# Top-k attention with a feed-forward block on one core: a first batch in single tiles, a regular conversion of the weights, and small operations put elsewhere

## The chip, the core and the metric

The kernel runs on one core of a Trainium2 chip. A core has five engines with a queue of instructions each, worked off in order: TensorE (PE in the profile; its weight loads are PEld), VectorE (DVE), ScalarE (ACT), GpSimd (POOL) and SyncE (SP), which here only issues DMAs. The metric is the time of one execution on the device, in microseconds (us). TensorE accumulates into PSUM; ScalarE copies from there to SBUF.

## The reference

There are 8 batches, 8 heads, 576 rows and 64 columns per head. Attention keeps, in every row of scores, those that are not below the 32nd largest. The result passes through a feed-forward block with a residual.

```python
scores = scale * np.matmul(q, k.transpose(0, 1, 3, 2))
kth = np.partition(scores, -top_k, axis=-1)[..., -top_k:-top_k + 1]
scores = np.where(scores >= kth, scores, -1000000000.0)
attn = np.exp(scores - np.max(scores, axis=-1, keepdims=True))
attn = attn / (np.sum(attn, axis=-1, keepdims=True) + 1e-09)
x = np.matmul(attn, v)            # then (B, H, S, D) -> (B, S, 512)
xn = (x - mu) / np.sqrt(var + 1e-06) * g_ln
out = x + np.maximum(xn @ w_ch1, 0.0) @ w_ch2     # 512 -> 2048 -> 512
```

The two weight matrices arrive as 64-bit floats, and the kernel converts them itself.

## The kernel before

**Units.** Two heads (a head pair `hp`, four of them) are worked on together. The 576 rows of queries are four tiles of 128 (`qt` 0 to 3) and a rest of 64 (`qt` = `J` = 4). A *unit* is one such tile of one head pair: two score tiles of 128 x 576, one per head; for the rest, one tile that holds both heads. A *job* is a batch, a head pair and a list of tiles. In batch 0 the lists are [0, 1] and [2, 3, J], from batch 1 on [0, 1, J] and [2, 3]; a list is done for all four head pairs before the next list. So there are 160 units in a fixed order.

**Steps.** The program is written as a loop over steps `n` (line numbers in the listing below), and there is no scheduler: each engine gets its instructions in the order in which the loop writes them. In step n, unit n is selected on VectorE, while its neighbours are at other stages:

- `scores` makes the scores of unit n+1 on TensorE (L362); ScalarE copies them from PSUM (L345).
- `select` finds the 32 largest of unit n in four rounds of MAX8 and MATCH_REPLACE8 (L379, L384). `select(u, 0)` to `select(u, 3)` stand at four places in the step; between them stands the other work.
- `prepare` and `mask` work on unit n-1: GpSimd adds a large negative number where a score is below the threshold (L409 compares, L412 adds). While weights are being converted, units are `shared`: for one of their two tiles ScalarE does the comparison (L399, L400), and GpSimd only subtracts (L407).
- `weigh` is the exponential of unit n-2 on ScalarE (L419), with the row sum into `den`; `turn` transposes it (L434, L463 on TensorE, copies L446 and L464).
- `values` multiplies the whole list by v when the list's last unit is n-3 (L487, L494; `oT`, L499), and `place` transposes back (`xo`, L526) and divides by `den` (`put`, L503, on ScalarE). The reciprocal of `den` is VectorE's (L782); an epsilon is added first, on GpSimd (L823).
- after the last head pair, `stats` takes mean and variance of the finished rows (L551, L552, VectorE), `std` the root (ScalarE), `inverse` the reciprocal (L561).

**Blocks.** Two finished row tiles are a block. `give` puts its matmuls into the list `todo`: `turn_x` (transposes, copied as `xT`, L576 and L581), 64 `hidden` (L589) and 32 `project` (L606), and each of the eight `fill` calls of a step pops as many as the plan's share allows, by estimated costs. The plan spreads a block over the steps up to the next block: windows of 12 and of 8 steps in turn. What is left then is popped at once. Behind the first list of batches 3 and 7 a second block comes on top, made of the rests of four batches.

**Weights.** Each of 32 *pieces* is fetched on SP, split by ScalarE into size, low part and sign (L168 to L172) and clamped on GpSimd (L173), shifted on VectorE (L176), and joined by two operations of GpSimd (L182, L183). Four pieces come before the loop, two in each of steps 0 to 9, and one a step until step 17. After four pieces of the first matrix `mean_of` forms a mean on TensorE and `centre` corrects the weights on VectorE (L223).

**Buffers** that matter: five PSUM banks `ps` for scores, transposes, `av` and `xo`; three `mm` for `hidden` and `project`; single input buffers `kin`, `qin`.

Of the kernel before, what the change touches and what calls it, by code (L numbers as in the profile page):

```python
# [20 lines left out]
J = 4  # L21
# [7 lines left out]
def kernel(  # L29
# [51 lines left out]
    NV = 3  # L81
# [19 lines left out]
    hpool = pool("h", NF - 1)  # L101
# [30 lines left out]
    class Piece:  # L132
# [26 lines left out]
        def split(self):  # L159
# [6 lines left out]
            self.sign = tmp("sign", FP32)  # L166
# [13 lines left out]
        def join(self):  # L180
            size = self.size[:]
            nc.gpsimd.tensor_tensor(size, size, self.low[:].bitcast(U32), ALU.add)  # L182
            nc.gpsimd.tensor_tensor(  # L183
                self.dst, size.bitcast(FP32), self.sign[:], ALU.mult
            )
            ready[self.i] = True

    ready = [False] * (2 * NF)
    centred = [False] * (DFF // DM)
# [3 lines left out]

    def load_gain():
        grow = const([NC, P], "grow")
        nc.scalar.dma_start(grow[:], g_ln.rearrange("(c p) -> c p", p=P))
# [23 lines left out]
    def centre(nb):  # L220
# [6 lines left out]
        centred[nb] = True  # L227
# [4 lines left out]
    for n in range(-1, 2 * NF):  # L232
        size = 4 if n < 0 else 2 if n < 10 else 1
        batches[n], queue = queue[:size], queue[size:]

    def weights(n, phase):

        now, before = batches.get(n, []), batches.get(n - 1, [])
        done = [x.i // NC for x in before if x.i < NF and x.c == NC - 1]
        if phase == 0:  # L240
            for x in batches.get(n + 1, []):
                x.fetch()
            for x in now[0::2]:
                x.split()
        elif phase == 1:
            for x in before:
                x.shift()
            for x in before[0::2]:
                x.join()
        elif phase == 2:  # L250
            for x in now[1::2]:
                x.split()
            for x in before[1::2]:
                x.join()
            for nb in means:
                if not centred[nb]:
                    centre(nb)
        elif phase == 3:
            for nb in done:
                mean_of(nb)  # L260
# [6 lines left out]

    def pop():
        cost, run, may = todo.pop(0)
# [4 lines left out]
    def fill():  # L274
        owed[0] = min(owed[0] + share[0], 6.0)
        while todo and owed[0] >= todo[0][0] / 2 and (not todo[0][2] or todo[0][2]()):
# [11 lines left out]
    def load(job, other):  # L288

        job.ins = {}  # L290
        for name, src, queue in (("k", k, nc.sync), ("q", q, other)):
# [47 lines left out]
    def scores(u):  # L339
# [3 lines left out]
        for s, pss in enumerate(made):  # L343
            for t, ps in enumerate(pss):
                nc.scalar.copy(u.sc[:, t, s * HALF : (s + 1) * HALF], ps[:, 0:HALF])  # L345
# [192 lines left out]
    class Block:  # L538
# [25 lines left out]
        def items(self):  # L564
# [38 lines left out]
            def project(i, f):  # L603
# [9 lines left out]
                if f == NF - 1:  # L613
# [7 lines left out]
            out = [(0.66, lambda i=i: turn_x(i), None) for i in range(n)]  # L621
            out += [
                (
                    max(per_row * N, 0.31),
                    lambda f=f, c=c: hidden(f, c),
                    lambda f=f: centred[f * P // DM],
                )
                for f in range(NF)
                for c in range(NC)
            ]  # L630
            out += [
                (
                    per_row * DM,
                    lambda i=i, f=f: project(i, f),
                    lambda f=f: ready[NF + f] and (f < NF - 1 or self.ready),
                )
                for i in range(n)
                for f in range(NF)
            ]
            return out  # L640

# [6 lines left out]
    for b in range(B):  # L648
        lo, hi = list(range(J // 2)), list(range(J // 2, J))
        (lo if b else hi).append(J)  # L650
        for qts in (lo, hi):
# [32 lines left out]
    for j in jobs:  # L684
        if j.hp == NHP - 1:
# [4 lines left out]
            add_block(step, tiles, [[(out[b, t[1] * P : (t[1] + 1) * P, :], full)] for t in tiles])  # L690
# [19 lines left out]
    turns = {}  # L710
    for j in fresh[1:]:
        before = jobs[jobs.index(j) - 1]
        turns[before.first] = j
# [21 lines left out]
    def give(n):  # L735
        while todo:
            pop()
        owed[0] = 0.0
        for blk in gives[n]:
            todo.extend(blk.items())  # L740
        after = [m for m in gives if m > n]
        steps = range(n, min(after) if after else END)
        need = sum(t[0] for t in todo)
# [7 lines left out]
    load(fresh[0], nc.scalar)  # L751
    weights(-2, 0)
    turn_heads(fresh[0])
    load(fresh[1], nc.sync)
    scores(units[0])
    load_gain()
    load_values(jobs[0])
    weights(-1, 0)
# [123 lines left out]
```

## Time and profile before

| | |
|---|---|
| median of three runs | 1772.06 us (1770.77 to 1772.45) |
| the profiled execution | 1770.78 us, span 1768.3 us |
| TensorE busy (PE) | 1635.9 us, 93% of the span |
| VectorE busy (DVE) | 1521.8 us, 86% |
| GpSimd busy (POOL) | 1208.3 us, 68% |
| ScalarE busy (ACT) | 969.3 us, 55% |
| a MAX8, a MATCH_REPLACE8 over 576 columns | 746 ns, 742 ns |
| the mask's comparison, its addition (GpSimd) | 2215 ns, 1409 ns |

The share of the span is a mean over stages with different limits, so the profile is read by stretches. A row of the windows view gives a stretch's start, end and length, and for each engine the busy time and the number of instructions, then the granted TensorE clock, the DMA share and GB/s. A line of a timeline gives start, duration, engine, line, operation, what is written and read, and in brackets the idle time before it and who ended it. In a waits line stand the total, the number of waits and the longest one.

### The profile page before, as it was taken

To read this page: it belongs to the slowest core of one execution; us is meant where nothing else is said; L and a number is where in the kernel's file an instruction comes from. 1 tells how busy PE (TensorE), PEld (TensorE's weight loads), DVE (VectorE), ACT (ScalarE), POOL (GpSimd) and SP (SyncE) were. 2 spreads that over 40 slices of the span, in tenths; PEclk is the share of its full clock that TensorE was granted. 3 is DMA by queue.
4 is the path that set the end of the run, shared out by engine and by line. 5 is a ranking of instruction groups with operands and counts; after the bars stand their busy time and mean duration, and the time that the engine had idled before them with its cause. 6 is when DMAs were issued, how large, how long until landed. Compare 5 with 4: busy or idle time off the path is not lost.

```text
span 1768.3 us, 23805 instructions
## 1 busy us (share of the span) xinstructions
PE 1635.9 (93%) x7617; PEld 1034.6 (59%) x7617; DVE 1521.8 (86%) x3162; ACT 969.3 (55%) x2563; POOL 1208.3 (68%) x959
## 2 busy tenths in 40 slices
PE   3555999999999999999999999999999999999998
PEld 1223746657574757575756575647575756566765
DVE  7888999999999999996569999999999999996000
ACT  4658876556564646553356565656565646544411
POOL 4869787787777777873467877777778776883300
PEclk9677999999999999999999999999999999999999
DMA  7423112101210012001021012101120021000000
GB/s 173 103 69 97 54 31 51 28 26 28 46 28 20 24 37 54 20 14 38 15 39 28 26 28 53 21 20 27 34 53 21 20 40 34 14 26 14 6 13 12
DMA packets 244485, 65.53 MB, mean 37 GB/s; under 512 B 235653, under 2 KB 235657, under 8 KB 244361
## 3 DMA queue, kind: packets, MB, share of 16 engines
q1 hardware_dynamic: 241984, 63.73, 16.2%
q8 instruction: 60, 0.98, 0.2%
q10 hardware_dynamic: 2376, 0.30, 0.1%
q14 instruction: 65, 0.52, 0.1%
HBM read 54.53 MB, written 9.44 MB: 36 GB/s over the span
## 4 chain that ended last, share of the span: by engine, by line
DVE 41%; PE 35%; POOL 9%; issue 9%; ACT 5%; DMA 1%; POOLq 0%; SPq 0%; DVEq 0%; ACTq 0%
DVE m L379 21%; DVE wk L384 18%; PE hps L589 13%; PE ops L606 11%; PE scps L362 4%; PE av L487 3%; PE tp L434 3%; POOL e L409 2%; POOL w L183 2%; POOL size L182 2%; POOL e L412 2%; ACT sc L345 1%; POOL e L407 1%; PE av L494 1%; POOL size L173 1%
## 5 line engine op out<-in xcount | busy, mean ns | idle before, releaser
L409 POOL TENSOR_SCALAR e<-sc,m 128x576 f32<-128x576 f32 x270 | 598.2, 2215 | 239.4 <-DVE m L379 170.9
L379 DVE MAX8 m<-wk 128x8 f32<-128x576 f32 x864 | 612.6, 746 | 2.1
L589 PE MATMUL hps<-xT,w 128*128 128x256 f32 x2304 | 556.9, 385 | 27.5 <-ACT xT L581 27.5
L606 PE MATMUL ops<-w,h 128*128 128x512 f32 x1152 | 544.0, 596 | 0.0
L589 PEld LDWEIGHTS hps<-xT,w 128*128 128x128 f32 x2304 | 419.5, 192 | 93.8 <-ACT xT L581 31.8
L384 DVE MATCH_REPLACE8 wk<-m,wk 128x576 f32<-128x576 f32 x576 | 423.7, 742 | 0.0
L412 POOL TENSOR_TENSOR e<-e,sc 128x576 f32<-128x576 f32 x270 | 380.3, 1409 | 22.6
L606 PEld LDWEIGHTS ops<-w,h 128*128 128x128 f32 x1152 | 199.3, 191 | 162.5 <-issue 157.4
L419 ACT ACTIVATE e<-e,bias 128x576 f32<-128x576 f32 x288 | 225.3, 782 | 57.5 <-POOL e L412 55.4
L345 ACT COPY sc<-scps 128x288 f32<-128x288 f32 x576 | 191.8, 415 | 97.9 <-PE scps L362 94.7
L379 DVE MAX8 m<-sc 128x8 f32<-128x576 f32 x288 | 203.1, 742 | 40.1 <-ACT sc L345 40.0
L362 PE MATMUL scps<-kT,qT 64*128 64x288 f32 (+3 forms) x1344 | 223.1, 435 | 9.3 <-DVE qT L321 8.1
L446 ACT COPY pt<-tp 128x512 f32<-128x512 f32 x256 | 150.3, 588 | 138.3 <-PE tp L434 136.8
L434 PE MATMUL tp<-ident,e 128*128 128x128 f32 x1152 | 178.0, 278 | 49.8 <-ACT e L419 49.8
L434 PEld LDWEIGHTS tp<-ident,e 128*128 128x128 f32 x1152 | 143.7, 143 | 126.7 <-ACT e L419 62.4
L384 DVE MATCH_REPLACE8 wk<-m,sc 128x576 f32<-128x576 f32 x288 | 211.9, 742 | 0.0
L362 PEld LDWEIGHTS scps<-kT,qT 64*128 64x128 f32 (+1 forms) x1344 | 126.5, 182 | 131.0 <-issue 59.7
L601 ACT ACTIVATE h<-hps 128x256 f32<-128x256 f32 x288 | 110.4, 384 | 159.5 <-PE hps L589 158.6
L487 PE MATMUL av<-pt,vb 128*64 128x256 f32 (+1 forms) x1024 | 141.2, 419 | 0.3
L616 POOL TENSOR_TENSOR o<-o,x 128x512 f32<-128x512 f32 x32 | 40.7, 1273 | 126.0 <-ACT o L615 125.7
L487 PEld LDWEIGHTS av<-pt,vb 128*64 128x64 f32 x1024 | 69.2, 139 | 66.5 <-issue 19.7
L503 ACT ACTIVATE x<-xo,den 128x64 f32<-128x64 f32 x256 | 59.3, 316 | 72.4 <-DVE den L782 39.2
(71 smaller groups left out, 1020.9 us busy)
## 6 DMA issues: line engine op xcount, KB each, us to landing
raw<-in_moe_w_ch_dram SPq DMA_DIRECT2D x32, 512.0 KB, 3.9
vb<-in_v_dram SPq DMA_DIRECT2D x128, 128.0 KB, 2.4
kin<-in_k_dram SPq DMA_DIRECT2D x128, 72.0 KB, 2.4
qin<-in_q_dram SPq DMA_DIRECT2D x124, 72.0 KB, 2.4
out_dram<-o SPq DMA_DIRECT2D x32, 256.0 KB, 2.1
ends<-in_v_dram SPq DMA_DIRECT2D x128, 16.0 KB, 2.1
dr<-den SPq DMA_DIRECT2D x64, 0.2 KB, 1.8
out_dram<-o SPq DMA_DIRECT2D x8, 128.0 KB, 2.4
```

What stands on the lines that cost most here:

```text
L345: nc.scalar.copy(u.sc[:, t, s * HALF : (s + 1) * HALF], ps[:, 0:HALF])
L362: nc.tensor.matmul(ps[i * R : i * R + ql, o : o + width], qT[r, q0 : q0 + ql], kT[r, k0 : k0 + width], start=True, stop=True,)
L379: nc.vector.max(m[:, t, :], u.cur[t])
L384: nc.vector.match_replace(u.wk[t][:], m[:, t, :], u.cur[t], LOWEST)
L409: nc.gpsimd.tensor_scalar(e, sc, u.thr[:, t, 7:8], MASKED, ALU.is_lt, ALU.mult)
L412: nc.gpsimd.tensor_tensor(e, e, sc, ALU.add)
L419: nc.scalar.activation(u.e[:, t], u.e[:, t], AF.Exp, bias=u.bias[:, t : t + 1], scale=scale, accum_out=g.den[:, col : col + 1],)
L434: nc.tensor.transpose(ps[:, c * P : (c + 1) * P], u.e[:, t, c * P + t * R : (c + 1) * P + t * R], ident[:],)
L446: nc.scalar.copy(g.pt[:, t * J : (t + 1) * J, q0 : q0 + P], ps[:].rearrange("p (c n) -> p c n", n=P),)
L487: nc.tensor.matmul(av[h * D : (h + 1) * D, 0 : g.nq], vb[:, h * J + c, :], g.pt[:, h * J + c, 0 : g.nq], start=(c == 0), stop=False,)
L589: nc.tensor.matmul(ps["h"][:, 0:N], w1[:, c, f * P : (f + 1) * P], xT[0][:, c, 0:N], start=(c == 0), stop=(c == NC - 1),)
L606: nc.tensor.matmul(ps["o"][:], hT[f][:, i * P : (i + 1) * P], w2[:, f, :], start=(f == 0), stop=(f == NF - 1),)
```

## The change

- **Order of batch 0.** The lists are [0], [1], [2, 3] and [J]; batch 1 has [0, 1] and [2, 3, J]; the later batches are as before. Batch 0 so has blocks of one tile (given in steps 7 and 11) and of two (step 19); the next come in steps 31 and 43, where before they came in 11, 23, 35 and 43.
- **Conversion.** None before the loop, then two pieces in every step 0 to 15; the shift moves behind the next step's `select(u, 0)`, the joins to phase 1, `mean_of` a step later. Units 0 to 15 are `shared`. A piece's sign lies in the `o` and `r` pools.
- **A readiness rule.** A block's matmul may be popped only in a step after the one in which its weights were made. While weights are missing, `give` doesn't empty `todo`, and puts new rows and `hidden` before the projections; later it may leave up to eight projections.
- **ScalarE and GpSimd.** Both exponentials of unit n-2 and `prepare` stand before `scores`; the copies go tile by tile; `mask` does both tiles at once, tile 1 first.
- **Small operations.** The epsilon is added on VectorE, and add and reciprocal stand behind `select(u, 1)` and the transposes of heads instead of behind `select(u, 0)`. `inverse` comes a step later.
- **Loads.** The first two jobs' heads are transposed before the loop, the others two steps ahead of their job; values are loaded near the end of a step, into two buffers instead of three.

```diff
-    NV = 3
+    NV = 2
-    hpool = pool("h", NF - 1)
+    hpool = pool("h", NF)
@@ weights
-        size = 4 if n < 0 else 2 if n < 10 else 1
+        size = 0 if n < 0 else 2
...
         if phase == 0:
             for x in batches.get(n + 1, []):
                 x.fetch()
+            for x in before:
+                x.shift()
             for x in now[0::2]:
                 x.split()
         elif phase == 1:
             for x in before:
-                x.shift()
-            for x in before[0::2]:
                 x.join()
-        elif phase == 2:
             for x in now[1::2]:
                 x.split()
-            for x in before[1::2]:
-                x.join()
+            for x in batches.get(n - 2, []):
+                if x.i < NF and x.c == NC - 1:
+                    mean_of(x.i // NC)
+        elif phase == 2:
...
+    def done(step):
+        return step is not None and step < now[0]
@@ jobs
-        lo, hi = list(range(J // 2)), list(range(J // 2, J))
-        (lo if b else hi).append(J)
-        for qts in (lo, hi):
+        parts = [[0], [1], [2, 3], [J]]
+        if b:
+            parts = [[0, 1], [2, 3]]
+            parts[b < 2].append(J)
+        for qts in parts:
@@ turns
-    turns = {}
-    for j in fresh[1:]:
-        before = jobs[jobs.index(j) - 1]
-        turns[before.first] = j
+    turns = {j.first - 2: j for j in fresh[2:]}
@@ give
-        while todo:
+        early = not all(map(done, ready))
+        while todo and not early and (len(todo) > 8 or todo[0][0] != "project"):
             pop()
...
+            kept = [i for i in todo if i[0] != "project"]
+            last = [i for i in todo if i[0] == "project"]
+            if early:
+                todo[:] = kept + rows + hidden + last + project
+            else:
+                todo[:] = kept + rows + last + hidden + project
...
+        if early:
+            plan.update({m: 1.2 for m in steps})
+            return
@@ the loop over steps
-        if u and n == u.job.first and n > 0:
-            load_values(u.job)
         if ex:
-            weigh(ex, 0)
+            for t in range(len(ex.tiles)):
+                weigh(ex, t)
+        if mk:
+            prepare(mk)
         if nxt:
             scores(nxt)
+        if n == 0:
+            load_gain()
         if g:
             values(g)
         if u:
             select(u, 0)
-        for den in recips.pop(n, []):
-            nc.vector.reciprocal(den, den)
         if mk:
-            prepare(mk)
-            mask(mk, 0)
+            for t in reversed(range(len(mk.tiles))):
+                mask(mk, t)
         weights(n, 0)
         fill()
-        if ex and len(ex.tiles) > 1:
-            weigh(ex, 1)
...
             turn_heads(turns[n])
...
+        for den in recips.pop(n, []):
+            nc.vector.tensor_scalar_add(den, den, DEN_EPS)
+            nc.vector.reciprocal(den, den)
         for blk in gives.get(n - 1, []):
             blk.std()
-        if mk and len(mk.tiles) > 1:
-            mask(mk, 1)
         weights(n, 1)
...
-        for blk in gives.get(n - 1, []):
+        for blk in gives.get(n - 2, []):
             blk.inverse()
...
-            nc.gpsimd.tensor_scalar_add(den, den, DEN_EPS)
...
+        if mk and mk.job.last == n - 1:
+            load_values(mk.job)
```

## The prediction

> **What bounds the kernel now.** I read the 40 slices first, then who waited for whom, then single steps. I call *step n* the stretch that begins with VectorE's first MAX8 on unit n (the row `m<-sc`). Steps 0, 20, 43, 54, 63 and 83 begin at 10.9, 257.7, 473.4, 570.0, 660.9 and 902.5 us.
>
> ```profile
> span 1768.3 us, 23805 instructions
> ...
> PE   3555999999999999999999999999999999999998
> ...
> DVE  7888999999999999996569999999999999996000
> ```
>
> TensorE starves for about 180 us. Then TensorE and VectorE are both full, except in two stretches where TensorE alone is (near 800 us and from 1575 us on). The same by steps (us, then PE, PEld, DVE, ACT, POOL busy, clock, DMA):
>
> ```profile
> 10.90:257.70 246.80, 159.28 (x662) 92.15 (x662) 220.62 (x429) 169.11 (x418) 188.73 (x160) 0.82 0.32 82
> 257.70:473.40 215.70, 209.83 (x1003) 130.16 (x1002) 213.41 (x451) 122.23 (x335) 167.52 (x131) 0.99 0.16 33
> 473.40:570.00 96.60, 94.53 (x467) 59.63 (x467) 96.08 (x200) 57.82 (x155) 72.20 (x58) 1.00 0.17 34
> 570.00:660.90 90.90, 89.22 (x432) 57.42 (x430) 88.64 (x189) 50.59 (x135) 70.08 (x51) 1.00 0.14 29
> 765.90:902.50 136.60, 135.72 (x595) 90.03 (x596) 82.26 (x175) 53.89 (x141) 65.17 (x48) 1.00 0.11 24
> ```
>
> So in steps 0 to 19 VectorE, the busiest engine, idles 26.2 us, nearly all of it explained by these waits of VectorE in that window:
>
> ```profile
> DVE den L782 <- POOL den L823: 21.1, 6, 6.1
> DVE size L176 <- POOL size L173: 2.8, 3, 1.4
> ...
> DVE w L223 <- PE mean L212: 1.6, 2, 1.1
> ```
>
> Later a batch's work comes in windows of 12 steps (VectorE is behind) and 8 steps (TensorE is behind). In the 12-step window TensorE gains a lead: the scores that it makes in step 55 start 8.0 us before VectorE's step 55. In the 8-step window the lead is used up, and VectorE stops before `st` (L551) for 1.95 us in step 62, and for 1.93, 2.77 and 1.93 us in steps 102, 122 and 142. What ends TensorE's lead is ScalarE's queue, here in step 54:
>
> ```profile
> 573.03 0.93 ACT L503 ACTIVATE x<-xo,den 128x64 f32<-128x64 f32 x4 [3.15 <-DVE den L782]
> 573.83 0.60 ACT L446 COPY pt<-tp 128x512 f32<-128x512 f32 x1
> 574.29 0.30 ACT L464 COPY pt<-tp 128x128 f32<-128x128 f32 x1
> 574.45 0.74 ACT L615 ACTIVATE o<-ops,rstd 128x512 f32<-128x512 f32 x1
> 575.03 0.82 ACT L419 ACTIVATE e<-e,bias 128x576 f32<-128x576 f32 x1
> ...
> 575.79 1.34 ACT L345 COPY sc<-scps 128x288 f32<-128x288 f32 x4
> 576.93 1.16 ACT L581 COPY xT<-tp 128x512 f32<-128x512 f32 x2
> ...
> 1572.00 3.29 PE L589 MATMUL hps<-xT,w 128*128 128x256 f32 x14 [1.22 <-ACT xT L581]
> ```
>
> The reader should see a chain: reciprocal of `den` (VectorE), `put`, copies, one exponential, score copies, `xT`, and only then TensorE may begin the next block (578.15 us, 8.15 after step 54 began; the last line is the same wait in step 154). From there to the window's end TensorE has no gap over 0.4 us, so a delay at this point moves the end one for one.
>
> **Part 1, steps 0 to 19.** *Goes:* the den add moves from GpSimd's queue to VectorE, `mean_of` comes a step later, shifts come after a full step. All 26 us of waits above lose their cause: -25.5 (21.1 + 2.8 + 1.6).
> *Start:* the second job's two transposes (0.75 each) now stand before the first MAX8. Their loads reuse the same buffers, so they are issued after the first transposes (4 issues of 0.5, landing 2.4 later). Step 0 begins near 14.0 instead of 10.9; the 1.4 us of transposes leave step 0: +1.7.
> *Shift (L176), 32 times, 0.905 us mean (0.384 to 1.629).* It is slow when GpSimd runs a two-input instruction: two shifts took 2.24 us beside `e` L407, a lone one 0.41 us beside the one-input `e` L409.
>
> ```profile
> 113.41 2.24 DVE L176 TENSOR_SCALAR size<-size 128x512 uint32<-128x512 uint32 x2
> ...
> 113.77 1.60 POOL L407 TENSOR_TENSOR e<-sc,e 128x576 f32<-128x576 f32 x1
> ...
> 247.65 0.41 DVE L176 TENSOR_SCALAR size<-size 128x512 uint32<-128x512 uint32 x1
> ```
>
> After the change both shifts stand 2.8 us into the step (after 2 MAX8 and 2 MATCH_REPLACE8). GpSimd starts the step with the mask of tile 1: one-input 2.22, two-input 1.41, then the two-input subtraction 1.41, so it is in two-input work from 2.3 to 5.1. I take 1.25 each: 32 x 0.345 = +11. Bounds: 0.42 each (-15.5), 1.5 each (+19).
> The Trainium skill ("SBUF — State Buffer", section "Who interferes with whom") says that the two engines share one port pair and the loser is blocked for the whole instruction, whichever GpSimd instruction it is; the 0.41 us shift beside L409 disagrees. By that rule a pair would take an estimated 2.9 us and the sum would be 6 us higher.
> *Small VectorE work:* 12 den adds and 5 more reciprocals at 0.17 (the reciprocal's row, 0.166): +2.9. The add on VectorE is in no row; bounds 0.08 (MATCH_VALUE_LOAD) and 0.23 (the same add on GpSimd).
> *TensorE:* blocks of one tile use 128 columns instead of 256 per `hidden`, at half the time each (four 128-column transposes take 0.44 in a run, eighteen 256-column instructions 3.89), so they cost no more in sum and lie in idle TensorE. But conversion now ends at step 16, so 16 projections fall into step 17: 16 x 0.86 (8 instructions, two to a projection, in 3.43) = 13.8 us in a 5.6 us step of a rest unit. TensorE begins step 17 about 2 us ahead and leaves it 14.5 us after VectorE's start; `place` and `put` of step 18 end 5 us later. VectorE wants these values for the `stats` of tiles 2 and 3 after 5.6 + 7.1 = 12.7 us: a wait of about 7 us (bounds 0 and 10). Steps 7 to 12, with up to 31 `hidden`: +1.
> *At nothing:* 8 more jobs of batch 0 mean 32 more value DMAs on SP at 0.5 us, and the loads go to the end of a step behind the weight fetches; used two steps (about 25 us) later, landing in 2.4. The queue could be late by a whole step before it costs. The second job's q loads on ScalarE's queue lie beside its wait for scores. Two `v` buffers instead of three: the old values are read at the start of the step in which the new load is issued.
> *Two tiles' statistics* come before step 20 instead of after: +1.7 here, -1.7 below. **Sum to step 20:** -25.5 + 1.7 + 11 + 2.9 + 7 + 1 + 1.7 = -0.2.
>
> **Part 2, steps 20 to 42.** VectorE sets the pace. The 8-step window of steps 35 to 42 becomes one of 12, so its final stall (1.2) goes; -1.7 from above; 11 adds at 0.17 less two reciprocals: +1.5. Sum -1.4; to step 43 **-1.6**. From step 43 on the block plan (which matmul is popped in which step) is the same.
>
> **Part 3, steps 43 to the end.** The reciprocal now stands behind the second MAX8 round, with the add ahead of it. In step 54 it is ready at 2.93 + 2.85 (a round) + 0.17 = 5.95 us instead of 2.93. ScalarE waits at `put`; behind it wait the copies, the scores' copies and `xT`. And both exponentials of a unit now stand ahead of the score copies: +0.86 more before `xT`. GpSimd masks tile 0 last (done 7.0 us into the step), earlier than ScalarE comes to it. So the next block starts 3.0 + 0.86 = 3.9 us later. TensorE would have been waiting. Its step 54 now starts 6.4 us before VectorE's; I lower that to 3.8, because in step 52, behind a rest unit, its first transposes must wait for tile 0's exponential (mask done 7.2 us after VectorE's end of that unit, 1.0 more for the exponential). `xo` stands 7.15 us into its step, so 3.4 us into VectorE's, 2.6 us before the den. In steps 74, 114 and 154 `put` was at 3.4 without a wait, so 3.5 there. Six such places (54, 74, 94, 114, 134, 154), after each of which TensorE is the bound: 3 x 3.9 + 3 x 3.5 = **+22.2**. Bounds: 0 (TensorE comes later than the den) and 33 (5.5 each, if the wait for both mask passes binds too).
> The adds in the six 12-step windows, 35 x 0.17 = **+6.0**; in 8-step windows they hide behind TensorE. For all 58 adds the bounds are -5 and +3.5. The Trainium skill ("VectorE: DVE Perf Modes", section "The TRN2 errata") gives 58 cycles plus the elements at 0.96 GHz, an estimated 0.065 us; by it the sum would be 6 us lower.
>
> Total -1.6 + 22.2 + 6.0 = +26.6. The profiled execution took 1770.78 (span 1768.3), 1.3 below the median of the three; 1770.78 + 26.6 = 1797.4. **Predicted: 1797 us**, own range 1784 to 1812.
>
> **Rivals.**
> *The start pays for all (not slower).* Place: the shifts of steps 1 to 16. If GpSimd runs so late that they meet its one-input work, they take 0.42 each: -15.5 instead of +11, so 1797 - 26.5 = 1771, no change. It decides below a mean shift of about 0.45. For it: 0.41 and 0.42 occur 8 times. Against: GpSimd had 58 us of idle there and will wait for VectorE at the start of each step.
> *The hand-overs cost nothing.* TensorE arrives later than the den or catches up: 1797 - 22 = 1775. Against: `put` waited 3.15 us in step 54 and VectorE already stops in 62, 102, 122 and 142.
> *Both:* 1749, faster.
> *Worse than summed:* shifts at 1.5, 5.5 per hand-over, 10 us in step 18: 1797 + 8 + 11 + 3 = 1819.
>
> **How the numbers follow.** Forecast 0.55; start alone 0.12; hand-overs alone 0.10; both 0.13; worse 0.10. A difference under 0.2% (3.5 us) can't be told from no change. Slower: 0.55 + 0.10 + 0.08 + 0.03 = 0.76. Same: 0.06 + 0.02 = 0.08. Faster: 0.13 + 0.03 = 0.16. The range 1752 to 1813 leaves out most of the worst and of the best case.
>
> **What would show it.** Step 20 within 10 us of 257.7, shifts above 1.1 us, a wait of VectorE in step 18. In steps 54, 94 and 134 `put` near 6.0 us into the step and `hps` starting near 12; waits before `st` of 5 to 6 us in steps 62, 102 and 142. If `hps` still starts near 8, the hand-over is wrong and the forecast is 22 us too high; if step 20 comes before 245, the start is.

## The result and the profile after

The changed kernel takes 1848.88 us (median of four runs, 1848.27 to 1850.94) against 1771.41 us in the same session: a ratio of 1.044, with an interval of 1.0422 to 1.0458. The direction was forecast, the size was not: 1797 us, with a range up to 1813.

The first lines of the page, and the two rows of its 40 slices:

```profile
span 1846.3 us, 24668 instructions
...
PE   3777889999899999999999999999999999999998
...
DVE  7999769999999999996559998999999998996200
```

Against before, TensorE's row shows a longer and denser start, and VectorE's row dips to 7 and 6 in its fifth and sixth slice (185 to 277 us). The windows view of the same steps as before (us, then PE, PEld, DVE, ACT, POOL busy, granted clock, DMA share, GB/s):

```profile
14.30:279.30 265.00, 188.43 (x957) 122.05 (x957) 232.71 (x449) 176.72 (x446) 199.63 (x161) 0.83 0.32 85
279.30:498.60 219.30, 201.56 (x992) 127.76 (x990) 217.66 (x454) 116.50 (x323) 158.20 (x115) 0.96 0.17 33
498.60:598.90 100.30, 94.93 (x447) 59.96 (x448) 99.47 (x206) 55.41 (x151) 70.56 (x53) 0.97 0.16 33
598.90:695.70 96.80, 94.24 (x439) 60.41 (x437) 90.48 (x194) 52.43 (x141) 69.56 (x47) 0.96 0.14 28
...
805.80:946.30 140.50, 138.73 (x599) 92.36 (x600) 85.06 (x179) 55.52 (x147) 63.89 (x44) 0.98 0.11 23
```

| stretch | before | after | difference | predicted |
|---|---|---|---|---|
| to step 20 | 257.7 | 279.3 | +21.6 | -0.2 |
| steps 20 to 42 | 215.7 | 219.2 | +3.6 | -1.4 |
| from step 43, where VectorE is the bound (43-53, 63-73, 83-93, ...) | 580.4 | 602.4 | +22.0 | +6.0 |
| from step 43, where TensorE is (54-62, 74-82, ..., 154 to the end) | 714.5 | 745.3 | +30.8 | +22.2 |
| span | 1768.3 | 1846.3 | +78.0 | +26.6 |

**The start.** In steps 0 to 19 VectorE works 12.1 us more than before (232.7 against 220.6), idles 6.1 us more (32.3 against 26.2), and step 0 begins 3.4 us later: 21.6 in sum. Of the three waits of before only the largest (21.1 us for the add) is gone, as predicted; the other two have grown, the one for the clamp from 2.8 to 8.3 us and the one for the mean from 1.6 to 3.2, and one in step 18 is new (VectorE's waits in that window: us in total, number, longest):

```profile
DVE st L557 <- ACT x L509: 15.7, 1, 15.7
DVE size L178 <- POOL size L175: 8.3, 4, 4.3
DVE m L385 <- ACT sc L349: 3.8, 1, 3.8
DVE w L227 <- PE mean L216: 3.2, 1, 3.2
```

The longest is the one in step 18. Its origin is on TensorE in step 17, which begins at 242.9 (timeline of TensorE, and the line of VectorE that waits):

```profile
245.96 2.07 PE L612 MATMUL ops<-w,h 128*128 128x512 f32 x2 [3.86 <-POOL w L185]
248.52 8.68 PE L612 MATMUL ops<-w,h 128*128 128x512 f32 x14 [0.49 <-POOL w L185]
...
272.06 0.69 DVE L557 BATCH_NORM_STATS2 st<-x 128x6 f32<-128x512 f32 x1 [15.69 <-ACT x L509]
```

TensorE meets the first projection before GpSimd has joined the weights for it (L185), loses 4.35 us to that, works off the projections until 265, and only then makes the scores, `av` and `xo` from which `x` comes. A part of this is the granted clock, the third value from the end of this row of the windows view:

```profile
243.20:253.40 10.20, 6.95 (x8) 2.67 (x9) 9.89 (x19) 2.89 (x7) 9.78 (x9) 0.50 0.01 2
```

Fourteen of the projections' instructions take 8.68 us, mostly in this stretch, 0.62 each; eight that follow at 257.48 take 3.60, 0.45 each.

A profile shows one execution. Three other kernels below are the same up to step 20 (E3, E5, E13); there step 20 begins at 279.9, 282.7 and 280.6, and the wait in step 18 is 17.0 to 17.3 us. Differences of 1 to 3 us in the start say little by themselves.

**The windows of VectorE.** The add on VectorE is the one new operation there (groups: count, then busy us, mean ns, idle before):

```profile
L821 DVE TENSOR_SCALAR den<-den 128x4 f32<-128x4 f32 (+1 forms) x68 | 36.7, 540 | 38.9 <-ACT e L425 38.9
...
L821 DVE TENSOR_SCALAR dr<-dr 128x2 f32<-128x2 f32 x16 | 8.0, 501 | 0.0
```

Its mean of 0.53 us is made of two kinds, as the timeline shows (VectorE, GpSimd, VectorE):

```profile
504.11 0.16 DVE L821 TENSOR_SCALAR dr<-dr 128x2 f32<-128x2 f32 x1
...
522.81 1.41 POOL L418 TENSOR_TENSOR e<-e,sc 128x576 f32<-128x576 f32 x1
...
523.40 0.85 DVE L821 TENSOR_SCALAR den<-den 128x4 f32<-128x4 f32 x1
```

The first add meets an idle GpSimd. The second begins inside GpSimd's two-input addition and ends with it (522.81 + 1.41 = 524.22; 523.40 + 0.85 = 524.25). Of the 84 adds 41 took over 0.5 us. Those in the stretches where VectorE is the bound took 19.8 us.

**The hand-over** of step 54, which now begins at 598.92 (ScalarE, ScalarE, ScalarE, TensorE):

```profile
604.92 0.93 ACT L509 ACTIVATE x<-xo,den 128x64 f32<-128x64 f32 x4 [4.09 <-PE scps L368]
...
608.45 1.33 ACT L349 COPY sc<-scps 128x288 f32<-128x288 f32 x4
609.59 1.16 ACT L587 COPY xT<-tp 128x512 f32<-128x512 f32 x2
...
610.80 2.08 PE L595 MATMUL hps<-xT,w 128*128 128x256 f32 x4 [0.76 <-ACT xT L587]
```

`put` is 6.0 us into the step and `hps` 11.9 (8.15 before); both stand where the prediction put them, and so they do in steps 74 to 154. The bracket of the first line names the matmuls of the scores, but the reciprocal ended at 604.83, just ahead of `put`, and the same line of steps 74, 114 and 154 names the reciprocal. From `put` to `xT` ScalarE has no idle time. VectorE's waits at the end of the stretches are where the prediction put them, too, here in steps 62 and 102:

```profile
694.10 0.69 DVE L557 BATCH_NORM_STATS2 st<-x 128x6 f32<-128x512 f32 x1 [5.77 <-ACT x L509]
...
1140.97 0.69 DVE L557 BATCH_NORM_STATS2 st<-x 128x6 f32<-128x512 f32 x1 [6.30 <-ACT x L509]
```

What the prediction did not have is the clock behind it (windows view; the granted clock is the third value from the end):

```profile
605.00:610.00 5.00, 3.29 (x14) 2.02 (x14) 4.96 (x11) 5.00 (x16) 4.15 (x6) 0.84 0.14 48
610.00:615.00 5.00, 4.24 (x13) 3.46 (x13) 4.97 (x12) 1.34 (x3) 4.84 (x3) 0.50 0.29 67
```

### The profile page after: what moved, and what is told of

Same layout as the page of the kernel before. It is cut to its first block, busy times and chain, and to the rows that moved or that the text cites. A ratio compares the mean times of both kernels' runs of the same rounds, so it can differ in the third digit from the quotient of the medians.

```text
span 1846.3 us, 24668 instructions
## 1 busy us (share of the span) xinstructions
PE 1684.9 (91%) x7889; PEld 1075.8 (58%) x7889; DVE 1571.8 (85%) x3251; ACT 968.6 (52%) x2582; POOL 1194.8 (65%) x882
## 4 chain that ended last, share of the span: by engine, by line
PE 41%; DVE 32%; issue 12%; ACT 7%; POOL 7%; DMA 1%; POOLq 0%; DVEq 0%; SPq 0%; ACTq 0%
DVE m L385 16%; PE hps L595 15%; PE ops L612 14%; DVE wk L390 12%; PE scps L368 4%; PE tp L440 3%; POOL e L415 3%; PE av L493 3%; POOL e L418 2%; ACT e L425 2%; ACT sc L349 1%; PE av L500 1%; DVE size L178 1%; DVE den L821 1%; ACT xT L587 1%
## 5 line engine op out<-in xcount | busy, mean ns | idle before, releaser
L415 POOL TENSOR_SCALAR e<-sc,m 128x576 f32<-128x576 f32 x272 | 603.7, 2219 | 330.3 <-DVE m L385 243.2
L595 PE MATMUL hps<-xT,w 128*128 128x256 f32 (+1 forms) x2432 | 576.4, 383 | 26.3 <-ACT xT L587 19.1
L612 PE MATMUL ops<-w,h 128*128 128x512 f32 x1152 | 551.2, 603 | 8.7 <-POOL w L185 8.7
L595 PEld LDWEIGHTS hps<-xT,w 128*128 128x128 f32 x2432 | 440.4, 198 | 95.6 <-ACT xT L587 23.9
L418 POOL TENSOR_TENSOR e<-e,sc 128x576 f32<-128x576 f32 x272 | 383.0, 1408 | 22.7
L368 PE MATMUL scps<-kT,qT 64*128 64x288 f32 (+3 forms) x1344 | 243.2, 433 | 69.4 <-DVE qT L325 41.9
L368 PEld LDWEIGHTS scps<-kT,qT 64*128 64x128 f32 (+1 forms) x1344 | 132.4, 178 | 198.8 <-issue 58.0
L440 PE MATMUL tp<-ident,e 128*128 128x128 f32 x1152 | 182.8, 284 | 31.9 <-ACT sc L349 21.0
L607 ACT ACTIVATE h<-hps 128x256 f32<-128x256 f32 (+1 forms) x304 | 113.7, 377 | 182.4 <-PE hps L595 181.3
L493 PE MATMUL av<-pt,vb 128*64 128x256 f32 (+3 forms) x1152 | 143.9, 392 | 2.3 <-DMA vb<-in_v_dram 2.3
L493 PEld LDWEIGHTS av<-pt,vb 128*64 128x64 f32 x1152 | 75.1, 140 | 66.4 <-issue 25.7
```

The costliest lines, as they stand in the source:

```text
L368: nc.tensor.matmul(ps[i * R : i * R + ql, o : o + width], qT[r, q0 : q0 + ql], kT[r, k0 : k0 + width], start=True, stop=True,)
L415: nc.gpsimd.tensor_scalar(e, sc, u.thr[:, t, 7:8], MASKED, ALU.is_lt, ALU.mult)
L418: nc.gpsimd.tensor_tensor(e, e, sc, ALU.add)
L440: nc.tensor.transpose(ps[:, c * P : (c + 1) * P], u.e[:, t, c * P + t * R : (c + 1) * P + t * R], ident[:],)
L493: nc.tensor.matmul(av[h * D : (h + 1) * D, 0 : g.nq], vb[:, h * J + c, :], g.pt[:, h * J + c, 0 : g.nq], start=(c == 0), stop=False,)
L595: nc.tensor.matmul(ps["h"][:, 0:N], w1[:, c, f * P : (f + 1) * P], xT[0][:, c, 0:N], start=(c == 0), stop=(c == NC - 1),)
```

## The experiments

Times are medians, ratios are to the kernel before of the same session (1770.8 to 1771.6), with their intervals. Edits are against the changed kernel where nothing else is said. "Behind step 43" is the length from the start of step 43 to that of step 159: 1155.5 before, 1208.3 after. E1, E7, E9 and E12 leave out the epsilon of the softmax's denominator.

### The small operations

**E1, no epsilon.**

```diff
-            nc.vector.tensor_scalar_add(den, den, DEN_EPS)
```

> The changed kernel without the epsilon: the add of 1e-9 to the softmax denominators is left out, so this part of the computation is missing; all else stands as it is. Theory A (the 84 adds on VectorE took 44.7 us in all, 0.84 to 0.92 each where GpSimd was in its two-input addition and 0.16 where it was not, and these waits are what makes the 12-step windows longer): the adds of steps 43 to 154 took 30.7 us; those in VectorE's windows come back whole, some 20 us, the hand-overs begin up to 0.8 us earlier, and a few us come back before step 43. Expected 1815 to 1825 against 1849. Rival B (the adds cost what a lone one costs, 0.16, and the windows are longer for another reason, such as ScalarE's order): 84 x 0.16 = 13 us at the most, so 1836 or more.

Measured: 1813.84 us, 1.0243 (1.0227 to 1.0258), 1.2 us below the range of A. The stretches in which VectorE is the bound return to 96.8 to 97.6 us from 99.3 to 101.1 (96.6 to 96.8 before), and steps 20 to 42 take 212.1 instead of 219.2. In sum those stretches are 582.1 us long, so that the add makes 20.3 of the 22.0 us in the table's third row, where 6.0 were predicted.

**E2, add and reciprocal back behind the first round of selection.**

```diff
             select(u, 0)
+        for den in recips.pop(n, []):
+            nc.vector.tensor_scalar_add(den, den, DEN_EPS)
+            nc.vector.reciprocal(den, den)
```

> The changed kernel with the add and the reciprocal put back behind the first round of MAX8, all else as changed. Theory A, for the hand-overs (the put of the denominators ends TensorE's lead in steps 54, 74, 94, 114, 134, 154): the reciprocal comes some 2 to 2.9 us earlier there, 6 x 2.0 to 2.9 = 12 to 17 us; and in steps of a rest unit the add falls into GpSimd's one-input work (0.16 instead of 0.84), which gives some 10 us more in the 12-step windows. Expected 1820 to 1832. Rival C (the hand-over waits for the two exponentials and not for the reciprocal): the place of the reciprocal makes no difference at the hand-over, and no more than the 10 us of the adds is seen: 1838 to 1850.

Measured: 1830.21 us, 1.0337 (1.0316 to 1.0358); behind step 43 1192.2, which is 16.1 less. That lies in the range of A, but not for its reason. The stretches where VectorE is the bound give 13.4 us, as their adds now take 6.7 us instead of 19.8; those where TensorE is give 2.6, where 12 to 17 were expected. `put` does come 1.7 us earlier (4.29 us into step 54), but `hps` only 0.3 (11.60), since ScalarE then waits for GpSimd's mask of tile 0 (ScalarE, ScalarE, TensorE):

```profile
598.06 0.93 ACT L509 ACTIVATE x<-xo,den 128x64 f32<-128x64 f32 x4 [1.81 <-DVE den L805]
...
601.54 0.77 ACT L425 ACTIVATE e<-e,bias 128x576 f32<-128x576 f32 x1 [1.04 <-POOL e L418]
...
605.37 0.92 PE L595 MATMUL hps<-xT,w 128*128 128x256 f32 x3 [1.22 <-ACT xT L587]
```

So the reciprocal is the last thing that the hand-over waits for in the changed kernel, but only by 0.3 us. The waits before `st` in steps 62 and 102 are gone and those of 122 and 142 fall to 2.7; in steps 54 to 62 VectorE is now busy for 93.7 of 94.4 us, and the adds of the stretches where TensorE is the bound rose from 12.7 to 25.8 us.

**E3, from step 20 on the add on GpSimd, the reciprocal behind the first round, the second exponential behind the first fill, all as before.** The order of the masks stays changed.

> The changed kernel in steps 0 to 19, and from step 20 on three of the moves undone: the add on GpSimd, the reciprocal behind the first round, the second exponential behind the first fill. The order of the two mask passes and of the score copies stays changed. Theory A (these three moves make the whole loss behind step 43, which was 52.8 us): 1849 - 45 to 55 = 1794 to 1804, with step 20 still at 279. Rival D (what comes behind step 43 is due to the new order of blocks, the masks or the loads): no more than half of it comes back, 1822 or more.

Measured: 1804.81 us, 1.0192 (1.0176 to 1.0208), just outside: behind step 43 1174.8, still 19.3 more than before, and waits before `st` of 4.65 and 4.64 us in steps 62 and 102. `hps` starts 10.86 us into step 54, still 2.7 later than before: something besides add, reciprocal and exponential delays the hand-over.

**E5, E3 and tile 0 masked first from step 20 on.**

```diff
-            for t in reversed(range(len(mk.tiles))):
+            for t in sorted(range(len(mk.tiles)), reverse=n < 20):
                 mask(mk, t)
```

> The kernel of the third experiment, and tile 0 masked ahead of tile 1 from step 20 on, as in the kernel before. Theory F (what was left of the loss behind step 43, 19.3 us by the steps, is the order of the masks: the exponential of tile 0 waits for both passes of GpSimd, so behind a rest unit, as in step 52, it ends 2.9 us into the step instead of 1.5 us ahead of it, and TensorE's lead falls by 2.8 us): about 2.5 us come back at each of six hand-overs: 1804.8 - 12 to 19 = 1786 to 1793. Rival G (the loads of values at the end of a step, the score copies by tile or the later inverse make what is left): 1800 to 1808.

Measured: 1788.09 us, 1.0097 (1.0082 to 1.0112); behind step 43 1154.0, as before, and `hps` 8.18 us into step 54. The order of the two masks is worth 20.8 us there, all of it in the stretches where TensorE is the bound. What is left of the loss lies ahead of step 43.

**E8, the other way round: the kernel before with the changed order of the small operations from step 20 on.**

> The kernel before, and from step 20 on the changed order of small operations alone: both exponentials and the bias ahead of the scores, both masks together with tile 1 first, add and reciprocal on VectorE behind the second round. Loads, blocks, conversion, copies and inverse as before. Theory A (this order is the whole loss behind step 43, whatever the start): 1771 + 45 to 60 = 1816 to 1831, with waits of VectorE of 5 to 7 us in steps 62, 102 and 142. Rival D (the loss needs the changed blocks or loads too): under 1805.

Measured: 1839.0 us, 1.0383 (1.0368 to 1.0399), above what was expected: steps 20 to 42 take 226.3 instead of 215.7, and behind step 43 it is 1212.4. With the start of before untouched (step 20 at 258.1) the order costs as much as in the changed kernel and more.

### The start

**E4, the shift just in front of its joins, where before had it.**

```diff
-            for x in before:
-                x.shift()
             for x in now[0::2]:
                 x.split()
         elif phase == 1:
+            for x in before:
+                x.shift()
             for x in before:
                 x.join()
```

> The changed kernel with the two shifts of a step moved from behind the first round of MAX8 to behind the second, just before the joins that need them. Theory A for the start (in steps 1 to 11 the shifts took 1.4 and 1.63 us because they meet two two-input instructions of GpSimd at a fixed place in the step): now GpSimd has only the join left, which waits for the shift, so the shifts take 0.42 each; 2.2 us less in some 11 steps, step 20 begins 15 to 25 us earlier than 279, and the time is 1824 to 1834. Rival E (GpSimd, not VectorE, sets the pace in steps 1 to 16, and the joins begin later now): step 20 within 6 us of 279 or later, 1843 or more.

Measured: 1840.23 us, 1.039 (1.0374 to 1.0405), between the theories. Step 16 begins 9.4 us earlier (224.0), but the wait in step 18 is 18.5 us (15.7 to 17.3 with the same start unchanged), and step 20 gains 6.5.

**E6, fewer projections popped in steps 17 and 18.**

```diff
-            plan.update({m: 1.2 for m in steps})
+            plan.update({m: 1.2 if m < 17 else 0.45 for m in steps})
```

> The changed kernel, with the share of the plan in steps 17 and 18 cut from 1.2 to 0.45, so that the 16 projections of step 17 are spread over several steps. Theory H (the 15.7 us that VectorE waits in step 18 are those projections, which stand ahead of the place and put of that step on TensorE): the wait falls to under 5 us, step 20 begins near 268 instead of 279.3, and 1849 - 8 to 13 = 1836 to 1841. Rival I (TensorE waits in step 17 for the last joins of GpSimd, and the projections behind them don't matter, or what is put off comes back in steps 20 to 31): 1845 or more.

Measured: 1842.93 us, 1.0407 (1.0392 to 1.0423), again between: the wait in step 18 falls from 15.7 to 11.8, and step 20 comes 6.9 earlier. A smaller share alone does not free step 17.

**E10, E5 with the lists of before in batches 0 and 1.** The new conversion stays.

```diff
-        parts = [[0], [1], [2, 3], [J]]
-        if b:
-            parts = [[0, 1], [2, 3]]
-            parts[b < 2].append(J)
+        parts = [[0, 1], [2, 3]]
+        parts[b < 1].append(J)
```

> The changed kernel with the order of the small operations of before from step 20 (as in the run at 1788.09), and with the lists of query tiles of before in the first two batches ([0, 1] and [2, 3, rest] for each), while the conversion keeps its two pieces per step behind the scores and the addition stays on VectorE in steps 0 to 19. M (the single tiles make the loss of the start: the projections of tiles 0 and 1 are all wanted before the statistics of step 18): the wait of 15.7 us before st falls below 6, step 20 starts at 262 to 270 instead of 282.7, and the time is 1768 to 1780. O (the conversion beside GpSimd and the shift's new place make it, whatever the lists): step 20 starts at 274 or later and the time is 1784 or more.

In the edit, as in before, batch 1 has [0, 1, rest] and [2, 3].

Measured: 1772.48 us, 1.0007 (0.9997 to 1.0016): no change against before. Step 20 begins at 264.2 instead of 282.7, and there is no wait before `st` in the start. The projections are as late in the step as in the changed kernel: TensorE waits 3.99 us for the joins in step 17, has clock 0.50 for 10.2 us and works on them until 256.5. But with these lists the statistics of tiles 2 and 3 stand in step 22 and not in step 18. The edit undoes two things, the single tiles and the separate list of the rest, and only the second moves these statistics; no run takes them apart.

**E11, E10 and the shift late.** The edit of E4 on top.

> The run with the old lists and the old order from step 20, and the shift of a piece moved from in front of the selection's fills to just in front of its joins, where before had it. If the shifts at their new place wait for GpSimd's two-input operations as in the changed kernel (1.41 and 1.63 us instead of 0.41): 5 to 10 us less than the run without this move, step 20 as much earlier. If the later joins hold the projections instead, as they did with the single tiles: within 3 us of it, with a longer wait before st in the steps up to 20.

Measured: 1759.73 us, 0.9935 (0.9918 to 0.9952), 0.65% faster than before, and more than was expected of it: 12.8 us below E10. Steps 0 to 19 of E10 in the windows view:

```profile
15.20:264.20 249.00, 173.60 (x673) 103.35 (x674) 231.69 (x434) 162.73 (x397) 194.03 (x157) 0.81 0.29 81
```

and its shifts in the groups of that window:

```profile
L178 DVE TENSOR_SCALAR size<-size 128x512 uint32<-128x512 uint32 x32 | 38.0, 1218 | 9.6 <-POOL size L175 9.6
```

The same two views of E11:

```profile
15.30:248.90 233.60, 172.22 (x674) 102.42 (x675) 217.56 (x435) 162.76 (x397) 192.93 (x157) 0.83 0.31 87
```

```profile
L178 DVE TENSOR_SCALAR size<-size 128x512 uint32<-128x512 uint32 x32 | 22.0, 722 | 5.2 <-POOL size L175 5.2
```

From the changed kernel to E10 VectorE's busy time hardly moves (232.7 to 231.7), its idle time falls from 32.3 to 17.3: the new lists cost idle time. From E10 to E11 the idle time stays (17.3 to 16.0), the busy time falls by 14.1, the shifts' by 16.0: the new place of the shift costs time in the shift itself. With the new lists the same move gave only 6.5 us at step 20 (E4); there TensorE waits 5.58 us for the joins in step 17.

### The clock

**E13, empty transposes at the hand-overs.** The edit is in `turn_x`:

```diff
+                again = (4, 2)[i] if now[0] >= 20 and n == 2 else 1
-                for c in range(NC):
+                for c in list(range(NC)) * again:
                     nc.tensor.transpose(
```

> The changed kernel, in which from step 20 on the four transposes of a block's first row tile (0.66 us) are made four times into the same PSUM tile, and those of its second tile twice. That is 2.0 to 2.2 us of empty TensorE work at every hand-over, most of it in the idle time that stands there anyway (1.22 us before the second tile, 0.76 us before the first hidden). C (part of the hand-overs' price is the granted clock: in the changed kernel it is 0.50 for 6.8 us from 9.5 to 11.1 us into steps 54, 74, 94, 114 and 134, with the idle time in TensorE as the cause, while step 154, with the same waits and full clock, lost 2.8 us instead of 4.5 to 6.7): the clock stays at 1.00 there, each of those stretches is 2 to 3 us shorter, and the time is 1833 to 1840. W (the clock falls for another reason, or doesn't cost anything): the half-clock spells stay or the stretches keep their lengths, and the time is 1847 to 1860 with the empty work on top.

Measured: 1842.54 us, 1.0405 (1.0388 to 1.0422): 6.3 us less than the changed kernel with more work in it, though 2.5 us above the range of C. The windows around the hand-over of step 54 (which begins at 600.15 here):

```profile
606.20:611.20 5.00, 4.48 (x30) 3.47 (x30) 4.97 (x11) 5.00 (x16) 4.18 (x6) 1.00 0.13 45
611.20:616.20 5.00, 4.22 (x22) 3.70 (x22) 4.96 (x12) 1.76 (x4) 4.84 (x3) 1.00 0.29 69
```

The clock stays at 1.00 in steps 54, 94, 114 and 134, and the stretches behind them take 94.66, 94.66, 94.78 and 94.66 us, where the changed kernel has 96.80, 97.08, 97.10 and 97.62: 2.1 to 3.0 us each. In step 74 a half-clock spell of 3.4 us is left, and that stretch is 1.0 us longer; the one behind step 154, which had kept its clock, pays 1.8 for the empty work. So filling TensorE's idle time keeps the clock up, and the spell costs 2 to 3 us at four of six places. That this is not chance shows in the other runs: where `hps` stands at 11.9 us without empty work (the changed kernel, E4, E6, E8), 22 of 24 hand-overs have a half-clock spell, in E13 one of six.

### Towards a faster version

**E7, the kernel before without epsilon.**

> The kernel before without the epsilon: the add of 1e-9 on GpSimd is left out (that part of the computation is missing; every denominator is at least 1, so in fp32 the sum is the same number). Theory A for the start of the kernel before (VectorE's 21.1 us of waits for this add in steps 4 to 16 are a cost of GpSimd's queue alone): step 20 begins 12 to 21 us earlier than 257.7, and the time is 1750 to 1760. Rival J (the wait is replaced by the next one, of VectorE for the shift or for GpSimd's masks, since GpSimd sets the pace): 1764 to 1772.

Measured: 1767.83 us, 0.9981 (0.9972 to 0.9991). Of the 21.1 us that VectorE waited for the add on GpSimd in the start, 5.7 come off at step 20; the next thing that it waits for is the clamp of the weights (VectorE's waits in steps 0 to 19 of E7, where before had 2.8 us in 3 waits):

```profile
DVE size L176 <- POOL size L173: 13.4, 8, 3.1
```

In the profiled execution (1770.32 us, of ten between 1764.56 and 1770.76) this gain is nearly gone by step 83 (step 94 begins at 998.5, before at 999.1): 2.7 us are lost in steps 20 to 30, with a wait of 2.43 us before `st` in step 22, and 1.7 us in steps 74 to 82, where this execution has a half-clock spell of 3.4 us and before had none.

**E9, E7 and the reciprocal in front of the first round from step 20 on.**

> The kernel before without the addition of epsilon (every denominator is a sum of exponentials of at least 1, so that 1e-9 lies below the rounding), and from step 20 on the reciprocal stands in front of the first round of selection, right behind the exponentials' step, instead of behind it. Nothing of the changed kernel is in it. K (the put of the weights, and so the hand-overs at steps 54, 94 and 134, end behind the reciprocal, which waits for a round of 2.7 us): the waits before st of 1.95 to 2.77 us in steps 62, 102, 122 and 142 go and some us of the TensorE-bound stretches with them; 1753 to 1762 against 1767.8 of the kernel without epsilon alone. L (the lead of TensorE over VectorE is set by the exponentials and the masks, not by the reciprocal): 1764 to 1772.

Measured: 1760.77 us, 0.9938 (0.9923 to 0.9953). The waits before `st` fall to 0.65, 1.00, 0.07 and 0.64 us in steps 62, 102, 122 and 142, `hps` starts 6.9 to 7.3 us into its steps (8.15 before), and no half-clock spell is left between steps 20 and 159. The reciprocal's place was a cost in the kernel before, too.

**E12, E11 with the edits of E9.**

> The run with the old lists, the late shift and the old order from step 20 (1759.73), without the addition of epsilon anywhere, and with the reciprocal in front of the first round of selection from step 21 on. What leaving epsilon out and moving the reciprocal took off the kernel before (10.8 us together, of which 5.1 lay before step 20, where before had its waits) should come off again, if the two changes act in different places: at least the 5.7 behind step 20, and in the start the contended additions of 0.9 us each, so 1746 to 1754. If the TensorE-bound stretches take back what comes earlier to them, as they did in the run of before without epsilon: 1756 to 1760.

Measured: 1753.98 us, 0.9904 (0.9887 to 0.992). At 5.75 us below E11 the time just reaches the range of the first theory, but not its terms: 3.8 us come off behind step 20, where at least 5.7 were expected, and 1.1 ahead of it. Behind step 43 it has 1149.9, 3.2 less. It is the fastest version here, 18 us below before and 95 below the changed kernel; of those that add the epsilon E11 is.

## Why the prediction was right or wrong

**The path from the changed kernel back** is a sum of four edits, each measured: 1848.9 less 44.1 (add, reciprocal and second exponential back, E3), less 16.7 (masks, E5), less 15.6 (lists, E10), less 12.8 (shift, E11) gives 1759.7. What is left in E11 of the change (two pieces per step behind the scores, the later `mean_of` and `inverse`, the turns and loads moved, two value buffers, the score copies by tile, both masks in one go, and in steps 0 to 19 the new order of the small operations) is a gain of 11.9 us (1771.6 less 1759.7): with the late shift and the old lists, step 20 begins at 248.9 instead of 257.7. Of the prediction's "All 26 us of waits above lose their cause" this much was right: the 21.1 us for the add are gone. VectorE's idle time in steps 0 to 19 falls by 10.2 us in E11 (26.2 to 16.0), not by 25.5.

**The failed step is the sum to step 20**, -0.2 against +21.6. The whole miss of 51.4 us (+78.0 against +26.6) is 21.8 there, 5.0 in steps 20 to 42, 16.0 where VectorE is the bound and 8.6 where TensorE is. By its own terms: the later start was right (3.4 us, put at 3.1). VectorE's work was put at +14.2 (shifts 11, small work 2.9, statistics 1.7, transposes -1.4) and was +12.1: the shifts took 34.3 us instead of 28.2, so +6 and not +11, while twelve adds took 5.3 us and with the reciprocals made +6.1 instead of +2.9. The idle time is what failed: put at -17.5 (-25.5 of waits, 7 in step 18 and 1 in steps 7 to 12), it was +6.1.
- The wait in step 18, "about 7 us (bounds 0 and 10)", was 15.7. The mechanism was right, but TensorE was taken to be limited only by its own work at full clock, and to leave step 17 14.5 us after VectorE had begun it. It left 22.1 us after (242.9 to 265.0): the wait of 4.35 us for GpSimd's joins and the half clock from 243.2 to 253.4 were not in the sum.
- The waits of 8.3 us for the clamp, 3.8 for scores and 3.2 for the mean had only the term of 1 us for steps 7 to 12. Why the clamp is late no run shows by itself (GpSimd now does two masks in one go ahead of it); E7 shows that the same wait stands ready in the kernel before as soon as the add is gone. The prediction removed waits without asking what is late next.

**The add** was put at 0.17 us, with bounds of 0.08 and 0.23, and cost 0.53 in the mean. The upper bound came from the same add on GpSimd. The prediction's own rows for the shift (2.24 us for two beside L407, 0.41 for a lone one) had the answer: a wait for the end of GpSimd's two-input operation doesn't depend on the size of what waits. The Trainium skill ("SBUF — State Buffer", section "Who interferes with whom") says that the loser is blocked for the whole instruction (of VectorE's operations those in a two-port mode); the add of 0.85 us that ends with L418 agrees; for GpSimd's comparison, which has one input, the 0.41 us shift of before still stands against it, and so does the add of step 54, 0.16 us long inside L415. One input is not what decides, though: shifts that meet the clamp of the weights (L175) end 0.28 us after it (0.61 and 0.77 us in steps 1 and 2 of E11). Even alone the add takes 0.16 us, not the estimated 0.065 that the prediction set beside its sum. VectorE's windows took 16.0 us more than predicted; E1 shows the add to make 14.3 of them, and in steps 20 to 42, where -1.4 was predicted, E1 takes 7.1 off the +3.6.

**The hand-overs** were right in place and in size: `put` at 6.0, `hps` at 11.9 in all six steps, 3.73 later than before, which makes 22.4 us in sum; the waits before `st` were 5.77, 6.30 and 6.78 us in steps 62, 102 and 142. The term that is missing is the clock. At full clock a hand-over costs 3.74 us (E13: 94.66 against 90.92, the empty work included) where 3.9 was predicted for steps 54, 94 and 134; the stretch behind step 154, with no half-clock spell, lost 2.8 where 3.5 stood. The 8.6 us above the predicted 22.2 are of the size of the five spells: E13 takes 9.8 us off four of those stretches.
That GpSimd masks tile 0 "earlier than ScalarE comes to it" held in the changed kernel, but only just: with the reciprocal back (E2) `hps` moves from 11.88 to 11.60 us and ScalarE waits for the mask; with the second exponential back too and the add on GpSimd (E3) to 10.86, with the order of the masks as well (E5) to 8.18. E3 and E5 differ in the masks alone, by 20.8 us behind step 43. The costs don't add: whichever is latest sets the hand-over, so undoing all but one leaves most of the loss. The exponential was never moved alone, so its own share stays open.

**The rivals.** That the start pays for all is out: the mean shift was 1.10 us, far above 0.45. That the hand-overs cost nothing is out by the lines of step 54. "Worse than summed" (1819) had the right sign. Of its three terms the shifts (1.5 each) did not come, the wait in step 18 passed its 10 us, and the hand-overs came near its 33 us with 30.8, but by the clock and not by the mask passes that it named. The add was not in it.

Open: how the gain of 11.9 us in E11 divides among the parts that stay in it; and why the clock kept full in step 154 of the changed kernel, whose waits on TensorE are like those of step 54. Two things in the traces bear on that. The spells of one profile begin whole multiples of 3.41 us apart (at the five hand-overs 608.4, 806.4, 1055.5, 1253.5 and 1451.5), so that the same gaps can fall into one such cell or be split between two. And the busy time of a cell alone does not decide: behind the first of these rows the clock falls, behind the second it doesn't.

```profile
605.00:608.40 3.40, 2.22 (x10) 1.30 (x10) 3.40 (x8) 3.40 (x11) 2.98 (x4) 1.00 0.00 0
1144.30:1147.70 3.40, 1.80 (x12) 1.32 (x11) 3.40 (x9) 3.34 (x9) 3.23 (x4) 1.00 0.42 122
```

## What to carry to other kernels

Price a tiny VectorE operation by what GpSimd does at that moment, not by its size: next to a two-input operation it costs the rest of that operation. Before a wait is booked as gain, look for what is late next on the same engine; here a wait of 21.1 us went, and the waits still rose from 25.5 to 31.0 us. When a late hand-over makes TensorE idle, look at the granted clock behind it, and when several things feed one hand-over, change all of them or none.

## What the runs showed of the hardware

- TensorE's granted clock fell to 0.50, for 3.4 or 6.8 us at a time, behind hand-overs where no single gap on TensorE was over 1.22 us (in step 54 gaps of 0.59, 1.22 and 0.76 us within 6 us, the spell beginning inside the second). The Trainium skill ("TensorE: Matmul & The Clock Gate", section "HAM oscillation — how this bites in real kernels") puts the rule as no idle gaps over about 3.4 us; the half clock and the spells' lengths agree with that page, the length of gap in this rule does not: the measurement shows that several short ones suffice, and not always (step 154).
- At half clock a `hidden` matmul has a median of 634 ns in step 54, against 379 ns in step 154 at full clock.
- An add over 4 columns takes 0.13 to 0.17 us beside an idle GpSimd, 0.16 us beside its comparison in step 54, and up to 1.40 us when it begins inside its two-input addition (L418).
- Thirty-two shifts of the same size took 38.0 (E10), 34.3 (changed), 28.2 (before) or 22.0 us (E11). The long ones end with an operation of GpSimd: in step 1 of the changed kernel 1.41 and 1.63 us, each 0.28 us behind the end of a two-input one.
